# Values of one attention step and scores of the next: from one joint TensorE block to two blocks with products between

## The chip, the cores and the metric

The kernel runs on 1 core of one Trainium2 chip. The metric is device time in microseconds; before the change three timed runs took 1113.95 to 1114.95 us, median 1114.69. A core has a TensorE (PE; its weight loads are listed as PEld), a VectorE (DVE), a ScalarE (ACT), a GpSimd (POOL) and a SyncE (SP) that issues transfers. Each has its own list of instructions and works through it in order; semaphores make one wait for another.

## The reference

Three parts follow each other: an attention over chunks of 32 rows, in which each chunk sees 16 rows to its left, itself, 8 rows to its right and 8 memory rows, and two layers of products.

```python
for c in range(nc):                       # 24 chunks of 32 rows; q: (4, 8, 768, 64)
    k_ctx = k[:, :, l_start:r_end]
    v_ctx = v[:, :, l_start:r_end]
    k_full = np.concatenate([mem_k, k_ctx], axis=2)
    v_full = np.concatenate([mem_v, v_ctx], axis=2)
    scores = scale * np.matmul(q_c, k_full.transpose(0, 1, 3, 2))
    a = np.exp(scores - np.max(scores, axis=-1, keepdims=True))
    a = a / (np.sum(a, axis=-1, keepdims=True) + 1e-09)
    out[:, :, c_start:c_end] = np.matmul(a, v_full)

x = attn_out.transpose(0, 2, 1, 3).reshape(3072, 512)
h = x @ w_in                              # 512 -> 2048
x = (h * np.tanh(softplus(h))) @ w_out    # 2048 -> 512
h = x @ w2_in
return (h * sigmoid(1.702 * h)) @ w2_out
```

## The kernel before

The 3072 rows are cut into 8 blocks of 384. Attention of block j + 1 and the first product of block j are worked on at the same time. The first product is `forward`: for block j and one of 16 column tiles it multiplies in 12 matmuls of 128x384 (each operand is cut into a high and a low part, three of the four cross products are kept), L1231 in the profile. These matmuls are called products below. Behind block 7 come `across` (L1494), `first` (L1393) and `second` (L1586), which the diff doesn't touch.

For blocks 0 and 1 attention works in other functions. From block 2 on one attention step is `duo`: two pairs of heads of one block, so two steps a block and 12 in all. A step is

- scores: 48 small fp32 matmuls in tiles of 64x32 (L1059), each of which the profile shows as two matmuls and two weight loads, into the banks `s0` and `o0`;
- softmax, once for each half `hh` of the heads: a memset (L1075), a maximum (L1076) and its scaling (L1078) on DVE, six exponentials on ACT (L1083), an inverse (L802, L805) and a multiply (L1095) on DVE, three PE transposes into `s1` or `o1` (L1103), and a copy out (L1109 or L1110);
- values: 48 small fp32 matmuls in tiles of 64x64 (L1123), shown as 96, into the banks `s1` and `o1`;
- evictions: the result into the high part of the next layer's input (ACT or DVE, L1135 and L1137), and the rest into the low part (DVE, L1139).

The queries and keys of a step are turned by DVE ahead of its scores (L668, L671, L675); the loads of `v` are issued by POOL (L374) into four tiles and wait for the values that free them.

Before the change the values of a step are not an operation of their own: `duo` hands them to the next step, whose scores operation runs them first and the scores behind them, without anything between. The planner sees one operation. The first step has scores alone, the last one's values stand alone, and in between are 11 joint blocks.

The order on every engine is made by `Plan`, a list scheduler in Python: each operation has a rank (its due time, counted in products' tiles of 12 matmuls), one or two engines that can do it, and a cost in microseconds. The planner steps through a simulated time, and an engine that is free takes the ready operation with the lowest rank. The constants at the top set ranks and costs: `VAL` is the rank of values behind the step's begin, `TURN` that of the first transposes, `LATE` the distance of the second half; `COSTS` and `COSTV` are the costs of scores and values. The instructions are then written out in that order.

Of the kernel before, what the change touches and what calls it, by code (L numbers as in the profile page):

```python
# [27 lines left out]
LATE = 3  # L28
TURN = 2.7
VAL = 7.2  # L30
COSTS = 0.95
COSTV = 0.85
COSTE = 0.43


# [31 lines left out]
def fixed(t=None):  # L67

    b = Buf(None, None, None)
    b.tile = t  # L70
    return b
# [219 lines left out]
def dve(n, fast=False):  # L291
    return (155 + (0.52 if fast else 1.046) * n) / 1000


def act(n, psum=False):
    return ((172 if psum else 200) + 0.835 * n) / 1000
# [7 lines left out]
def kernel(  # L304
# [733 lines left out]
        add(r + 2.7, [("pe", 1.0 + 0.75 * (len(kept) - 1), values)], reads=reads, writes=writes)  # L1038
        evict()

    def duo(j, hp0, heads, r0, before):

        reads, writes = [x for pair in heads for x in pair], []
        cost, rank = COSTS, r0 + 0.5
        if before:
            last, rank, given, made_by, finish = before
            reads, writes, cost = reads + given, made_by, cost + COSTV
        s = [T[n].new([P, GR, 2, KEYS], F32) for n in ("s0", "o0")]

        def scores():  # L1050
            if before:
                last()
            for i, (qT, kT, _) in enumerate(heads):
                keys = kT.get().rearrange("p c d -> p (c d)")
                for c in range(NCH):
                    g, c0 = divmod(c * CHUNK, P)
                    for hh in range(2):
                        d = slice(hh * D, (hh + 1) * D)
                        nc.tensor.matmul(  # L1059
                            out=s[hh][c0:c0 + CHUNK, g, i], lhsT=qT[d, c * CHUNK:(c + 1) * CHUNK],  # L1060
                            rhs=keys[d, c * BLK:c * BLK + KEYS], start=True, stop=True, tile_position=(hh * D, c0),
                        )

        add(rank, [("pe", cost, scores)], reads=reads, writes=writes + s)
        if before:
            finish()

        vt = [values_of(j, 2 * hp0 + hh, r0) for hh in range(2)]
        left = j * TB % S == 0
        row, g, k0, n = (0, 0, 0, LEFT) if left else (P - CHUNK, GR - 1, KEYS - RIGHT, RIGHT)  # L1070

        def softmax(hh, r):
            e = T["e"].new([P, GR, 2, KEYS], F32)
            mx, sm, iv = (T[x].new([P, GR, 2], F32) for x in ("mx", "sm", "r"))
            add(r + 0.5, [("dve", 0.16, lambda: nc.vector.memset(s[hh][row:row + CHUNK, g, :, k0:k0 + n], NEG))], updates=[s[hh]])  # L1075
            add(r + 0.6, [("dve", dve(TB), lambda: nc.vector.tensor_reduce(  # L1076
                out=mx.get(), in_=s[hh].get(), axis=mybir.AxisListType.X, op=ALU.max))], reads=[s[hh]], writes=[mx])
            add(r + 0.6, [("dve", 0.16, lambda: nc.vector.tensor_scalar(  # L1078
                out=mx.get(), in0=mx.get(), scalar1=-scale, scalar2=None, op0=ALU.mult))], updates=[mx])
            done = fixed()  # L1080

            def power(g, i):
                nc.scalar.activation(  # L1083
                    out=e[:, g, i], in_=s[hh][:, g, i], func=AF.Exp, scale=scale,
                    bias=mx[:, g, i:i + 1], accum_out=sm[:, g, i:i + 1],
                )

            for g_ in range(GR):
                for i in range(2):
                    add(  # L1090
                        r + 1, [("act", COSTE, lambda g=g_, i=i: power(g, i))],
                        reads=[s[hh], mx], writes=[done, sm, e], table="exp",
                    )
            inverses(r, sm, iv)
            add(r + 1.4, [("dve", dve(TB), lambda: nc.vector.tensor_tensor(  # L1095
                out=e.get(), in0=e.get(), in1=iv.get().unsqueeze(3).to_broadcast([P, GR, 2, KEYS]), op=ALU.mult,
            ))], reads=[iv, done], updates=[e])
            t = T[("s1", "o1")[hh]].new([P, TB], F32)
            aT = T["aT"].new([P, TB], F32)

            def turn():
                for g in range(GR):
                    nc.tensor.transpose(  # L1103
                        t[:, g * P:(g + 1) * P], e[:, g].rearrange("p i k -> p (i k)"), ident.get()
                    )

            add(r + TURN, [("pe", 0.43, turn)], reads=[e, ident], writes=[t])
            add(r + TURN + 0.2, [
                ("act", act(TB, True), lambda: nc.scalar.activation(out=aT.get(), in_=t.get(), func=AF.Copy)),  # L1109
                ("dve", dve(TB), lambda: nc.vector.tensor_copy(out=aT.get(), in_=t.get())),  # L1110
            ], reads=[t], writes=[aT])
            return aT

        aT = [softmax(hh, r0 + LATE * hh) for hh in range(2)]
        o = [T[n].new([P, TB], F32) for n in ("s1", "o1")]

        def values():
            for c in range(NCH):
                cs = slice(c * CHUNK, (c + 1) * CHUNK)
                for hh in range(2):  # L1120
                    for i in range(2):
                        d = slice(i * D, (i + 1) * D)
                        nc.tensor.matmul(  # L1123
                            out=o[i][hh * D:(hh + 1) * D, cs], lhsT=vt[hh][d, c], rhs=aT[hh][d, cs],
                            start=True, stop=True, tile_position=(i * D, hh * D),
                        )

        def evict():
            if j not in x0:
                x0[j] = Inputs("xh", j), Inputs("xl", j)  # L1130
            xh, xl = x0[j]
            for i in range(2):
                hp, part = hp0 + i, fixed()
                add(r0 + VAL + 0.2, [
                    ("act", act(TB, True), lambda hp=hp, i=i: nc.scalar.activation(  # L1135
                        out=xh.at(hp), in_=o[i].get(), func=AF.Copy)),
                    ("dve", dve(TB), lambda hp=hp, i=i: nc.vector.tensor_copy(out=xh.at(hp), in_=o[i].get())),  # L1137
                ], reads=[o[i]], writes=[xh.buf(hp), part])
                add(r0 + VAL + 0.4, [("dve", dve(TB), lambda hp=hp, i=i: nc.vector.tensor_tensor(  # L1139
                    out=xl.at(hp), in0=o[i].get(), in1=xh.at(hp), op=ALU.subtract))],  # L1140
                    reads=[o[i], part], writes=[xl.buf(hp)])

        reads = [*vt, *aT]
        if (j, hp0) != (NB - 1, H // 2 - 2):
            return values, r0 + VAL, reads, o, evict
        add(r0 + VAL, [("pe", COSTV + 0.1, values)], reads=reads, writes=o)
        evict()

    def quads():

        last, todo, before = None, [], None
        for j in range(NB):
            if j == EARLY:
                more = [T[x].new([P, 2 * DM], F32) for x in ("wo15", "wo11", "wo12", "wo13", "wo14")]
# [15 lines left out]
            for n in range(NQ):  # L1170
                rank = base + 2 * n
                if j == 0:
                    gp, hp = divmod(n, H // 2)
                    if hp == 0:
                        st = rows_of_heads(j, gp, rank)
                    heads, vals = turned(j, hp, gp, st, rank), st[2]
                else:
                    hp, gp = divmod(n, GB // 2)
                    if gp == 0:
                        if j >= EARLY:  # L1180
                            todo.append(pair_of_heads(j, hp, rank - 4 * (hp % 2)))
                            if hp % 2:
                                before = duo(j, hp - 1, todo, rank - 4, before)
                                todo = []
                            yield
                            continue
                        if hp == 0:
                            st = [rows_of_heads(j, i, rank) for i in range(GB // 2)]
                        pair = [turned(j, hp, i, st[i], rank) for i in range(GB // 2)]
                        names = (("s0", "s1"), ("o0", "o1"))[hp % 2]  # L1190
                        s = oct_scores([pair], rank, [names])[0]
                        both = [T[x].new([GQ, GB, 2], F32) for x in ("sm", "r")]
                        es = [quad(j, hp, i, pair[i], rank + STAGGER * i, s, both) for i in range(GB // 2)]
                        inverses(rank + STAGGER, *both)
                        for _, scaled in es:
                            scaled()
                        oct_out(j, rank, [x[2] for x in st], [(hp, names, [e for e, _ in es], 0)])
                    yield
                    continue
# [536 lines left out]
```

## Time and profile before

| | |
|---|---|
| median of three timed runs | 1114.69 us |
| profiled execution, its own time | 1113.29 us |
| its span (first to last instruction) | 1111.5 us |
| PE busy | 1079.9 us (97%) |
| DVE busy | 796.3 us (72%) |
| ACT busy | 552.4 us (50%) |
| mean granted clock of PE | 0.994 of full speed |

A stretch of the views is given in microseconds from the first instruction. In rows of busy time by stretch the columns are the stretch, its length, the busy time and the count of instructions of PE, PEld, DVE, ACT and POOL, the granted clock of PE as a share of full speed, the share of the DMA engines' time, and GB/s. In rows in order of time they are the start, the length, the engine, the line and operation, the tiles written and read. In the chain of waits a row is a piece of the chain that ended last, and "issue" is time in which the engine waited for nothing that the profile shows. A row of waits names the engine and line that waited, what it waited for, the total, the number of times and the longest.

### The profile page before, as it was taken

The numbers are of one execution on the slowest core, as the hardware profiler recorded it, in microseconds if no ns is written. First come the engines' busy times: TensorE is split into PE (matmuls) and PEld (weight loads), VectorE is DVE, ScalarE is ACT, GpSimd is POOL, SyncE is SP. The second block draws the span as 40 slices with busy tenths as digits, with TensorE's granted clock in tenths as the row PEclk, the third lists the DMA queues.
The fourth block names the chain that finished last, engine by engine and source line by source line (L and its number), as shares of the span: only waits on it lengthen the run. The fifth ranks groups of instructions, "written<-read, shape, count | busy, mean of one in ns | idle before, by whom it ended". The sixth has DMA issues, their size and how long they took to land.

```text
span 1111.5 us, 24805 instructions
## 1 busy us (share of the span) xinstructions
PE 1079.9 (97%) x9642; PEld 1045.3 (94%) x9642; DVE 796.3 (72%) x1457; ACT 552.4 (50%) x1247; POOL 98.4 (9%) x167
## 2 busy tenths in 40 slices
PE   7899899999999999999999999999999999999998
PEld 6568898998999999999999999999999999999998
DVE  5995654746545698898879865667556787877875
ACT  5874444444454464655555556555565533333332
POOL 2006443235300000000000000000000000000000
PEclk9999999999999999999999999999999999999999
DMA  9988998789876764754642777868678636445361
GB/s 178 274 233 211 250 224 232 202 226 243 239 246 233 249 190 159 252 162 136 220 146 83 223 244 239 289 219 285 212 251 253 182 101 171 115 125 151 104 162 48
DMA packets 278732, 221.28 MB, mean 199 GB/s; under 512 B 113552, under 2 KB 253867, under 8 KB 278615
## 3 DMA queue, kind: packets, MB, share of 16 engines
q1 hardware_dynamic: 272055, 209.46, 64.2%
q0 software_dynamic: 6560, 10.24, 3.7%
q8 instruction: 76, 1.25, 0.5%
q14 instruction: 41, 0.34, 0.1%
HBM read 138.33 MB, written 81.26 MB: 198 GB/s over the span
## 4 chain that ended last, share of the span: by engine, by line
PE 85%; DMA 5%; DVE 5%; issue 2%; SPq 2%; ACT 1%; DVEq 0%; ACTq 0%
PE o L1231 13%; PE h L1231 12%; PE o L1586 9%; PE o L1494 8%; PE h L1393 8%; PE o L1393 6%; PE h L1586 6%; PE s L1494 6%; PE s L1586 5%; PE h L1494 5%; PE s L1393 3%; DMA st<-wd 2%; SPq L374 2%; PE s L1123 1%; PE s L1059 1%
## 5 line engine op out<-in xcount | busy, mean ns | idle before, releaser
L1231 PE MATMUL o<-xh,wi 128*128 128x384 f32 x320 | 85.0, 347 | 0.0
L1231 PE MATMUL h<-xh,wi 128*128 128x384 f32 x320 | 82.4, 338 | 0.0
L1231 PEld LDWEIGHTS o<-xh,wi 128*128 128x128 f32 x320 | 58.1, 192 | 0.7 <-issue 0.3
L1231 PEld LDWEIGHTS h<-xh,wi 128*128 128x128 f32 x320 | 57.7, 188 | 0.6 <-ACT z L1363 0.2
L1231 PE MATMUL o<-xl,wi 128*128 128x384 f32 x160 | 54.5, 341 | 0.0
L1231 PE MATMUL h<-xl,wi 128*128 128x384 f32 x160 | 53.7, 336 | 0.0
L1363 ACT ACTIVATE e<-h 128x384 f32<-128x384 f32 (+2 forms) x47 | 22.4, 476 | 46.8 <-PE h L1586 28.8
L1586 PE MATMUL o<-wo,xh 128*128 128x256 f32 x232 | 43.7, 282 | 0.0
L1576 DVE TENSOR_TENSOR xl<-vt,xh 128x1024 fp32r<-128x1024 f32 x24 | 29.4, 1223 | 19.6 <-ACT xh L1573 17.5
L1576 DVE TENSOR_TENSOR xl<-wi,xh 128x1024 fp32r<-128x1024 f32 x32 | 38.8, 1223 | 5.8 <-ACT xh L1573 5.0
L1494 PE MATMUL o<-xh,wo 128*128 128x256 f32 x224 | 40.5, 282 | 0.0
L1231 PE MATMUL o<-wo,wi 128*128 128x384 f32 x192 | 38.7, 351 | 0.0
L374 POOL DMA_DIRECT2D vt<-in_v_dram x50 | 32.4, 652 | 64.5 <-PE o L1123 33.0
L1573 ACT ACTIVATE xh<-wi 128x1024 fp32r<-128x1024 f32 x25 | 26.4, 1057 | 22.8 <-DMA wi<-gd 12.5
L374 POOL DMA_DIRECT2D wo<-in_v_dram x50 | 32.0, 644 | 65.1 <-PE o L1123 64.4
L1477 DVE TENSOR_TENSOR xl<-z,xh 128x1024 fp32r<-128x1024 f32 x24 | 29.3, 1223 | 9.5 <-ACT xh L1473 8.9
L1586 PEld LDWEIGHTS o<-wo,xh 128*128 128x128 f32 x232 | 36.0, 190 | 0.0
L1231 PE MATMUL h<-wo,wi 128*128 128x384 f32 x192 | 35.1, 337 | 0.0
L1231 PEld LDWEIGHTS o<-wo,wi 128*128 128x128 f32 x192 | 34.6, 196 | 0.4
L1494 PEld LDWEIGHTS o<-xh,wo 128*128 128x128 f32 x224 | 34.6, 190 | 0.0
L1363 ACT ACTIVATE ev<-o 128x384 f32<-128x384 f32 (+2 forms) x32 | 15.1, 471 | 39.1 <-PE o L1586 17.2
L1231 PEld LDWEIGHTS h<-wo,wi 128*128 128x128 f32 x192 | 33.7, 189 | 0.0
(462 smaller groups left out, 3502.2 us busy)
## 6 DMA issues: line engine op xcount, KB each, us to landing
st<-in_moe_w_out_dram SPq DMA_DIRECT2D x32, 512.0 KB
st<-wd SPq DMA_DIRECT2D x29, 512.0 KB
z<-g1d SPq DMA_DIRECT2D x24, 512.0 KB
vt<-gd SPq DMA_DIRECT2D x24, 512.0 KB
wi<-gd SPq DMA_DIRECT2D x24, 512.0 KB
g1d<-gl SPq DMA_DIRECT2D x46, 192.0 KB
g1d<-z SPq DMA_DIRECT2D x45, 192.0 KB
wi<-in_moe_w_in_dram SPq DMA_DIRECT2D x16, 512.0 KB
```

What stands on the lines that cost most here:

```text
L374: queue.dma_start(out=o, in_=i)
L1059: nc.tensor.matmul(out=s[hh][c0:c0 + CHUNK, g, i], lhsT=qT[d, c * CHUNK:(c + 1) * CHUNK], rhs=keys[d, c * BLK:c * BLK + KEYS], start=True, ...
L1123: nc.tensor.matmul(out=o[i][hh * D:(hh + 1) * D, cs], lhsT=vt[hh][d, c], rhs=aT[hh][d, cs], start=True, stop=True, tile_position=(i * D, h ...
L1231: nc.tensor.matmul(out=h.get(), lhsT=a[:, c], rhs=b.at(kk), start=(n == 0), stop=(n == KD * len(prods) - 1))
L1363: ("act", act(n, True), lambda: nc.scalar.activation(out=dst(), in_=bank.get(), func=AF.Copy)),
L1393: nc.tensor.matmul(out=bank.get(), lhsT=a, rhs=b, start=(fresh and m == 0), stop=(m == 3 * K2 - 1), skip_group_check=not fresh,)
L1477: add(rank + 0.05, [("dve", dve(n2), lambda gh=gh, gl=gl, src=src: nc.vector.tensor_tensor(out=flat(gl), in0=flat(src), in1=flat(gh), op=A ...
L1494: nc.tensor.matmul(out=bank[:, d, :], lhsT=a, rhs=b[:, p, :], start=(fresh and h == d == p == m == 0), stop=(h == 1 and p == HP - 1 and m ...
L1573: ("act", act(NP * P), lambda: nc.scalar.activation(out=flat(gh), in_=flat(src), func=AF.Copy)),
L1576: add(rank + 0.05, [("dve", dve(NP * P), lambda: nc.vector.tensor_tensor(out=flat(gl), in0=flat(src), in1=flat(gh), op=ALU.subtract))], re ...
L1586: nc.tensor.matmul(out=bank.get(), lhsT=a[:, p], rhs=b, start=(fresh and p == 0 and m == 0), stop=(p == NP - 1 and m == 2), skip_group_che ...
```

## The change

`duo` gets the values and their evictions as operations of its own, at rank `VAL` behind the step's begin, and its scores at rank `SCORE` = 1.5 behind it instead of 0.5 or, joined with the values before them, at those values' rank. The costs are 1.05 for scores and 1.75 for values, instead of 0.95 and 0.85, 1.80 for a joint block. Nothing is computed otherwise.

```diff
-COSTS = 0.95
-COSTV = 0.85
+SCORE = 1.5
+COSTS = 1.05
+COSTV = 1.75
...
-    def duo(j, hp0, heads, r0, before):
-
-        reads, writes = [x for pair in heads for x in pair], []
-        cost, rank = COSTS, r0 + 0.5
-        if before:
-            last, rank, given, made_by, finish = before
-            reads, writes, cost = reads + given, made_by, cost + COSTV
+    def duo(j, hp0, heads, r0):
+
+        reads = [x for pair in heads for x in pair]
         s = [T[n].new([P, GR, 2, KEYS], F32) for n in ("s0", "o0")]
 
         def scores():
-            if before:
-                last()
             for i, (qT, kT, _) in enumerate(heads):
...
-        add(rank, [("pe", cost, scores)], reads=reads, writes=writes + s)
-        if before:
-            finish()
+        add(r0 + SCORE, [("pe", COSTS, scores)], reads=reads, writes=s)
...
-        reads = [*vt, *aT]
-        if (j, hp0) != (NB - 1, H // 2 - 2):
-            return values, r0 + VAL, reads, o, evict
-        add(r0 + VAL, [("pe", COSTV + 0.1, values)], reads=reads, writes=o)
-        evict()
+        add(r0 + VAL, [("pe", COSTV, values)], reads=[*vt, *aT], writes=o)
+        if j not in x0:
+            x0[j] = Inputs("xh", j), Inputs("xl", j)
...
-                                before = duo(j, hp - 1, todo, rank - 4, before)
+                                duo(j, hp - 1, todo, rank - 4)
```

Through ranks and costs the planner's order changes on all engines between the first scores and the first rows of `across`. In the new kernel scores are L1054, transposes L1096, values L1116 and products L1218.

PE before, in the middle of the joint block of the fifth and sixth step (at 178 to 184 us in the trace): the last values of one step (L1123) and the first scores of the next (L1059).

```order
L1123 MATMUL s_2534<-z_267,vt 64x32
L1123 MATMUL o_2536<-z_267,vt 64x32
L1059 MATMUL s_2584<-wo_945 32x64
L1059 MATMUL o_2586<-wo_945 32x64
L1059 MATMUL s_2584<-wo_945 32x64
```

PE now, at the same two blocks: the last values, the products (L1218) of two column tiles, the first scores.

```order
L1116 MATMUL o_2491<-z_267,vt 64x32
L1218 MATMUL h<-wo_1504,wi_942 128x384 x2
L1218 MATMUL h<-wo_1510,wi_942 128x384
...
L1218 MATMUL h<-wo_1753,wi_984 128x384 x2
L1218 MATMUL h<-wo_1760,wi_984 128x384
L1054 MATMUL s_2593<-wo_945 32x64
L1054 MATMUL o_2595<-wo_945 32x64
```

24 products stand between the two now; so it is in eight places.

PE now, between the first values (L1116) and the third scores (L1054).

```order
L1116 MATMUL o_1440<-z_267,vt 64x32
L1218 MATMUL h<-xh,wi_697 128x384 x2
L1218 MATMUL h<-xl,wi_697 128x384
L1218 MATMUL h<-xh,wi_697 128x384 x2
L1218 MATMUL h<-xl,wi_697 128x384
L1054 MATMUL s_1513<-wo_945 32x64
```

Only 6 products stand here. The second scores moved to between the first step's two groups of transposes.

PE now, between the third values and the fourth scores.

```order
L1116 MATMUL s_1865<-z_267,vt 64x32
L1116 MATMUL o_1867<-z_267,vt 64x32
L1054 MATMUL s_1922<-z_152 32x64
L1054 MATMUL o_1924<-z_152 32x64
L1054 MATMUL s_1922<-z_152 32x64
```

At this place the planner still puts the scores right behind the values.

DVE before, behind the scores of that sixth step: the memsets (L1075), the low parts of the values before (L1139), the two maxima (L1076).

```order
L1137 CAST xh<-s_2534 128x384
L1075 MEMSET s_2584 32x2x16
L1075 MEMSET o_2586 32x2x16
L1139 TENSOR_TENSOR xl<-s_2534,xh 128x384
L1139 TENSOR_TENSOR xl<-o_2536,xh 128x384
L1076 TENSOR_REDUCE mx<-s_2584 128x6
L1076 TENSOR_REDUCE mx<-o_2586 128x6
```

DVE now, at the same place (L1130 and L1132 are the evictions, L1068 the memsets, L669 and L672 transposes of later queries and keys, L1069 the maxima).

```order
L1130 CAST xh<-o_2491 128x384
L1132 TENSOR_TENSOR xl<-s_2489,xh 128x384
L1132 TENSOR_TENSOR xl<-o_2491,xh 128x384
L669 STREAM_TRANSPOSE z_152<-z_136 128x384
L1068 MEMSET s_2593 32x2x16
L1068 MEMSET o_2595 32x2x16
L672 STREAM_TRANSPOSE wo_945<-wo_383 128x13x32
L1069 TENSOR_REDUCE mx<-s_2593 128x6
L1069 TENSOR_REDUCE mx<-o_2595 128x6
```

The evictions moved from between memset and maximum to ahead of the memsets.

## Rows read from the trace of the kernel before

**Rows 1.** The page: busy times; the instruction queue's packets, MB, share
```profile
PE 1079.9 (97%) x9642; PEld 1045.3 (94%) x9642; DVE 796.3 (72%) x1457; ACT 552.4 (50%) x1247; POOL 98.4 (9%) x167
...
q8 instruction: 76, 1.25, 0.5%
```

**Rows 2.** Busy by stage: stretch, length, PE, PEld, DVE, ACT, POOL, clock, DMA share
```profile
88.00:330.00 242.00, 231.09 (x3433) 223.06 (x3432) 138.61 (x377) 110.99 (x424) 91.34 (x150) 0.98 0.89 232
...
520.00:1111.50 591.50, 584.51 (x4266) 581.97 (x4265) 432.00 (x609) 279.55 (x480) 0.00 (x0) 1.00 0.59 181
```

**Rows 3.** What PE waited for, 88 to 332 us: total, times, longest
```profile
PE s L1059 <- issue: 7.4, 4, 2.5
PE o L1059 <- issue: 3.5, 3, 1.5
```

**Rows 4.** Chain of waits, two joint blocks: start us, us, what
```profile
119.47 0.17 PE s L1123
121.37 2.17 issue
...
124.44 3.32 PE o L1231 x18
...
158.02 0.17 PE s L1123
...
160.66 2.28 PE o L1231 x12
```

**Rows 5.** Busy time and instruction counts between stalls, columns as in rows 2
```profile
108.33:119.30 10.97, 10.97 (x127) 10.68 (x126) 8.46 (x26) 5.59 (x29) 7.07 (x13) 1.00 1.07 242
119.30:123.54 4.24, 2.07 (x126) 1.78 (x126) 0.56 (x1) 0.49 (x1) 1.51 (x3) 1.00 0.96 245
178.80:183.15 4.35, 1.81 (x138) 1.62 (x130) 0.56 (x1) 0.87 (x2) 3.17 (x6) 1.00 0.96 241
247.63:250.24 2.61, 1.95 (x141) 1.76 (x133) 0.56 (x1) 0.87 (x2) 1.06 (x2) 1.00 0.40 89
183.15:250.24 67.09, 66.43 (x886) 64.91 (x885) 40.73 (x105) 31.89 (x117) 20.58 (x35) 0.97 0.81 209
```

**Rows 6.** Chain of waits: products behind three stalls, behind values alone, later
```profile
140.44 2.22 PE o L1231 x6
...
183.57 3.84 PE o L1231 x12
...
269.58 3.58 PE o L1231 x12
...
330.12 4.36 PE o L1231 x24
334.48 4.16 PE h L1231 x24
```

**Rows 7.** Busy time and granted clock behind the stall that ended at 139.15
```profile
140.44:142.66 2.22, 2.22 (x7) 2.22 (x8) 2.16 (x8) 0.00 (x0) 2.06 (x4) 0.50 1.29 182
```

**Rows 8.** Chain of waits: first products behind three steps' scores
```profile
109.21 4.38 PE o L1231 x24
...
205.41 2.30 PE o L1231 x12
...
313.88 1.25 PE o L1231 x6
```

**Rows 9.** Order of time on DVE, five places: start us, us, instruction
```profile
93.66 0.20 DVE L675 COPY wo<-z 128x96 f32<-128x96 f32 x1
...
114.11 0.20 DVE L675 COPY z<-z 128x96 f32<-128x96 f32 x1
...
205.41 0.55 DVE L1139 TENSOR_TENSOR xl<-o,xh 128x384 fp32r<-128x384 f32 x1
...
210.56 0.56 DVE L1095 TENSOR_TENSOR e<-e,r 128x384 f32<-128x384 f32 x1
...
325.52 0.56 DVE L1095 TENSOR_TENSOR e<-e,r 128x384 f32<-128x384 f32 x1
```

More of the change, by code (lines that the diff above doesn't have):

```diff
@@ L1126, in values @@
                         )
[L1128 to L1141, printed above, removed]
-        reads = [*vt, *aT]
-        if (j, hp0) != (NB - 1, H // 2 - 2):
-            return values, r0 + VAL, reads, o, evict
-        add(r0 + VAL, [("pe", COSTV + 0.1, values)], reads=reads, writes=o)
-        evict()
+        add(r0 + VAL, [("pe", COSTV, values)], reads=[*vt, *aT], writes=o)
+        if j not in x0:
+            x0[j] = Inputs("xh", j), Inputs("xl", j)
+        xh, xl = x0[j]
+        for i in range(2):
+            hp, part = hp0 + i, fixed()
+            add(r0 + VAL + 0.2, [
+                ("act", act(TB, True), lambda hp=hp, i=i: nc.scalar.activation(
+                    out=xh.at(hp), in_=o[i].get(), func=AF.Copy)),
+                ("dve", dve(TB), lambda hp=hp, i=i: nc.vector.tensor_copy(out=xh.at(hp), in_=o[i].get())),
+            ], reads=[o[i]], writes=[xh.buf(hp), part])
+            add(r0 + VAL + 0.4, [("dve", dve(TB), lambda hp=hp, i=i: nc.vector.tensor_tensor(
+                out=xl.at(hp), in0=o[i].get(), in1=xh.at(hp), op=ALU.subtract))],
+                reads=[o[i], part], writes=[xl.buf(hp)])
     def quads():
-        last, todo, before = None, [], None
+        last, todo = None, []
         for j in range(NB):
```

## The prediction

> **What bounds the kernel now.** I read the page's busy line, then the busy time by stage, then what TensorE (PE) waits for in the stage that changes, then the chain of waits through that stage, and last the instruction counts between its stalls.
>
> PE is busy 97% of the span [rows 1]. By stage it is busy 231.1 of 242.0 us between 88 and 330 us, where the changed blocks run, and 584.5 of 591.5 us from 520 us to the end [rows 2]. So microseconds that PE loses or gains between 88 and 330 us go to the end nearly one for one, unless something else becomes late. What PE waits for in that stage is one thing: 10.9 us (7.4 + 3.5) in seven pieces, all at the scores' matmuls of L1059 and all called "issue" [rows 3]. No piece is a wait for data.
>
> The chain shows where such a piece lies. One joint block begins with values at 119.47, goes over to scores, and in the middle of the scores PE stands for 2.17 us; products go on at 124.44. The undisturbed block goes from 158.02 to 160.66, 2.64 us, against 4.97 here [rows 4]. There are 11 joint blocks; 7 have such a stall and 4 do not, as the seven pieces say.
>
> The stalls have a period. Between the stall that ends at 108.33 and the one that ends at 123.54, PE ran 127 + 126 and 126 + 126 matmuls and weight loads, and between those that end at 183.15 and 250.24 there are 886 + 885 [rows 5]: 253, 252 and 7 x 253. The page's instruction queue moved 76 packets and 1.25 MB, and PE alone has 2 x 9642 such instructions [rows 1], which is 254 a packet. So I take it that PE stands because the next packet of its own instructions has not come: a stall sits at a packet's boundary. Counted on in this way along PE's list, eight of the 11 joint blocks meet two boundaries, one just ahead of the block or in its values and one in its scores; seven of these eight stall, and the three blocks with one boundary don't. How long a packet takes after the boundary before it: 252 instructions took 4.24 us with the stall, in other blocks 4.35 and 2.61 us [rows 5]. A joint block is 384 matmuls and weight loads in 2.64 us, so a whole packet is used up there in under 2 us; products (24 in 4.16 us [rows 6]) use one up in 22 us.
>
> The Trainium skill, "Runtime: NRT & Kernel Launch", section on instruction fetch mechanics, names blocks of 16 KiB (256 instructions), which fits the count, and calls the cost of crossing one "mostly hidden". By that sentence the stalls would not be fetches, the change would win nothing and the time would be that of the first rival below; the trace disagrees with it here, with 10.9 us in seven pieces.
>
> **What the change removes.** Values and scores become two blocks. In PE's new list 24 products stand between them in eight of the eleven places, 6 in one and none in one; the second values stand alone among products. The price of the stalls, all of it:
> - standing: 10.9 us [rows 3].
> - restart: the block above is 2.33 us longer than the undisturbed one, of which 2.17 is standing; 0.16 x 7 = 1.1 us.
> - clock: behind three stalls the granted clock is down, in the one shown 0.50, the 1.2 GHz level [rows 7]. Twelve products take 3.84 and 3.58 us and six take 2.22, against 2.28 for twelve behind the undisturbed block [rows 4, 6] (six: 2.28 less six at 4.16/24, 1.24). Lost: 1.56 + 1.30 + 0.98 = 3.8 us.
>
> Sum 15.8 us. Which of it stays follows from where the boundaries fall in the new list, counted on in packets from the first scores, up to which PE's list is unchanged. With 24 products between, the shortest way from one boundary to the next holds 4.16 us of products and about 1.3 us of small matmuls, 5.5 us, over the longest packet time seen (4.35). Two places are shorter. With 6 products between (first values, third scores) a packet holds some 124 instructions of values, 6 products and 119 of scores, about 2.9 us: a wait of 0 to 1.5 us, I take 0.7. Where values and scores still touch (third values, fourth scores) it holds 174 and 82, about 1.85 us: a wait of 0 to 2.5 us, I take 1.4, the mean of the eight old blocks with two boundaries (10.9 / 8), and add 0.16 for the restart and 0.55 for the clock (three of seven stalls lost 1.3 each). Stays: 2.8 us.
>
> **What it adds.** A seam each time PE goes from small tiles back to products: behind values that stand alone 24 products take 4.36 us instead of 4.16 [rows 6], 0.2 us; going in shows no extra piece in the chain. Ten new seams, 2.0 us.
>
> **What it moves.** PE's work is otherwise the same, and so are the instructions of VectorE (DVE) and ScalarE. Two moves matter.
>
> First, the softmax has less time. Until now 42 to 54 products stood between the scores and their first transpose; now 36 in four steps (6.2 us, with the seam 6.4) and 42 to 54 in the next five, with 12 or 6 more before the second transpose (8.9 us behind the scores in the four steps, 9.9 to 11.0 in the five). The DVE multiply that the first transpose needs ended 5.7 us behind the scores in an undisturbed step (205.41 to 210.56 + 0.56), and the slowest second one 12.2 us behind (313.88 to 325.52 + 0.56) [rows 8, 9]. So the bounds are no wait at all and, if every second multiply were as slow as that one, 3.3 x 4 + 2.3 + 2.2 + 1.2 x 3 = 21.3 us. But in the old list the evictions of the joint block's values stood ahead of the reduce on DVE; in the new one they come 24 products earlier, which takes two subtractions of 0.55 us out of the softmax's way [rows 9]. The undisturbed row is the nearer one, and its slack is 0.7 us: I take 1.0 us for all nine steps.
>
> Second, early scores move forward. The second scores stand right behind the first step's first transposes now, and behind the first values the third scores come after 6 products (1.0 us) instead of after the second scores, 54 products, transposes and the second values (1.1 + 9.4 + 0.6 + 1.5 us): 11 to 12 us sooner each. Their DVE copies ended at 93.86 and 114.31 in the old run [rows 9]. The third's overwrite tiles that the second scores read until 109.21 [rows 8], so it was PE that dated them; now those tiles are free that much sooner. Cost 0, at most about 5 us (114.31 against the 109 at which the third scores now come due) if the loads are the true date, and no gain is in it, since PE has products to do meanwhile.
>
> DMA must bring the same bytes in a stage 10 us shorter: 0.89 of 242 us [rows 2] becomes 0.93. No PE wait there is for a load, so I cost it at nothing; if the cover is gone the stage can give back no more than it won.
>
> **Sum.** 15.8 - 2.8 - 2.0 - 1.0 = 10.0 us faster. The profiled execution took 1113.29 us, its span 1111.5; the difference of 1.8 lies around it. It stands 1.4 us below the median of the three timed runs, 1114.69. 1113.29 - 10.0 = 1103.3 for such a run, 1104.7 for the median. This leaves PE's waits behind the stage as they are.
>
> **Rivals.**
> - The stalls are not PE's instructions, or PE's queue delivers them as late in any order (the change doesn't do what it says). For it: four joint blocks run without one. Against it: the period of 253, and that the blocks without a second boundary never stall. Then nothing goes, seams and waits are added: 1114.7 + 2.0 + 1.0 = 1117.7. Chance 0.05. The skill's "mostly hidden" would come out here too.
> - Fetches get slower, or more boundaries fall badly than I count, and half of the stalls stay: 1114.7 - 7.9 + 3.0 = 1109.8. Chance 0.08.
> - Loads date the third and fourth scores: up to 5 us come back, 1110. For it: DMA is at 0.89 of the stage and the scores are pulled forward by 12 us. Against it: no PE or DVE wait for a load there. Chance 0.12.
> - Slower: PE waits for the softmax. Place: the second transpose of the nine steps from the fourth scores on; price, if each second multiply ends as late as the slowest shown, the 21.3 us above in place of my 1.0: 1114.7 - 11.0 + 21.3 = 1125. It decides from 1.2 us a step (11.0 / 9). For it: 0.7 us of slack is little, and DVE takes other work between the softmax's instructions. Against it: the evictions leave the way, the slowest row is that of one step only, the last, and PE has no such wait now [rows 3]. Chance 0.05.
>
> **How the numbers follow.** The forecast has 0.70; its own range is 1100 (no stall stays and no wait is added: 1114.7 - 15.8 + 2.0 = 1100.9) to 1109. The two rivals at 1110 hold 0.20 more, and with them the range is 1100 to 1112. A change under 0.2% (2.2 us) can't be told from none by a measurement of this kernel. Faster: 0.70 + 0.08 + 0.12, less 0.05 for both of these together, which would eat the gain: 0.85. Same: those 0.05. Slower: the first rival and the last, 0.10.
>
> **What would show it.** Right: PE's "issue" waits between 88 and 330 us fall from 10.9 to 1 to 4 us, and the rest sits where 6 products or none separate the blocks; the granted clock in the stage rises from 0.98 to 0.99 or more; 24 products more stand behind the last values now, so these end about 14 us earlier, near 316 us; products behind a block alone take 0.2 us more. Wrong: "issue" pieces with 24 products around them; PE waiting at L1096 (the new transposes) for DVE, or at L1054 for DVE's copies; or the last values early and the end not, which would put the loss into the waits behind 330 us.

## The result, and the profile after

The changed kernel takes 1103.5 us (median of six runs, 1101.3 to 1105.1), the kernel before 1114.8 beside it (1113.3 to 1117.6). The ratio is 0.990, 95% interval 0.988 to 0.991: faster by 11.3 us; a second measurement (experiment 7) has 0.993, 7.3 us. Predicted were 1104.7 us and a range of 1100 to 1112. The profiled execution of after took 1105.1 us, the longest of the six, its span 1103.3.

The page of after, its busy line and its instruction queue; they answer [rows 1].

```profile
PE 1079.3 (98%) x9642; PEld 1041.1 (94%) x9642; DVE 800.3 (73%) x1456; ACT 555.8 (50%) x1246; POOL 98.6 (9%) x169
...
q8 instruction: 76, 1.25, 0.5%
```

PE has the same instructions and the same busy time to 0.6 us, in a span 8.2 us shorter. Busy time by stretch in after, columns as in [rows 2]. The first row is the stage, from the first scores to the end of the products before the last values; the three others answer to [rows 5] and run from one packet boundary to the next, with 277, 277 and 282 matmuls and weight loads begun or running in them (254 to 256 begin there, the others were still running).

```profile
89.91:318.98 229.07, 223.67 (x3313) 212.62 (x3312) 141.49 (x376) 113.47 (x423) 91.38 (x152) 1.00 0.92 246
108.52:112.27 3.75, 3.09 (x142) 2.65 (x135) 3.72 (x10) 1.37 (x3) 2.37 (x4) 1.00 0.87 170
133.26:136.37 3.11, 2.06 (x139) 1.88 (x138) 1.59 (x3) 1.34 (x3) 1.36 (x3) 1.00 0.63 208
299.20:305.27 6.07, 5.83 (x145) 5.37 (x137) 3.56 (x7) 2.59 (x5) 0.00 (x0) 1.00 1.08 380
```

The granted clock of the stage is 1.00 now, against 0.98, and DMA is at 0.92 against 0.89 [rows 2]. What PE waited for between 84 and 332 us in after; it answers [rows 3]: line, releaser, total, times, longest.

```profile
PE s L1096 <- DVE e L1088: 1.5, 1, 1.5
PE s L1054 <- issue: 1.3, 2, 1.0
PE o L1096 <- ACT z L1350: 1.0, 1, 1.0
PE o L1096 <- DVE e L1088: 0.8, 2, 0.5
PE o L1054 <- issue: 0.7, 1, 0.7
```

The unexplained "issue" falls from 10.9 us in seven pieces to 2.0 in three. In its place PE waits 3.3 us at the transposes (1.5 + 1.0 + 0.8), where it did not wait before. The chain of waits of after shows the three pieces and, at its end, the products behind the last values; it answers [rows 4, 6].

```profile
109.63 1.25 PE h L1218 x6
...
111.61 0.66 issue
...
133.20 0.17 PE s L1116
...
134.73 0.17 PE s L1054
...
135.32 1.05 issue
...
305.03 0.24 issue
...
320.58 4.36 PE h L1218 x24
324.95 4.16 PE o L1218 x24
```

The piece of 0.66 us stands in the scores behind the place with 6 products, that of 1.05 where values (133.20) run into scores (134.73) without a product, and that of 0.24 at a place with 24 products.

What such a piece waits for can also be read directly, since the trace lists the transfers of the instruction queue: 76 packets of 16 KB in a run. The rows show that queue from 121.00 to 122.10 us in before, ahead of the stall that ends at 123.54, and from 302.80 to 303.90 us in after, ahead of the piece that ends at 305.27 (packets, MB, share of the DMA engines' time).

```profile
q8 instruction: 1, 0.02, 5.8%
```

```profile
q8 instruction: 1, 0.02, 5.6%
```

No other packet of the queue begins between the packet boundary ahead of the stall and the stall's end. The first packet takes 1.02 us and ends at 122.05, the second takes 0.98 us and ends at 303.85; PE goes on 1.49 and 1.41 us later. The same holds for all 32 pieces of "issue" in the stage in the twelve profiles of this case: PE goes on 1.2 to 1.6 us after the end of such a packet, though packets come only every 9 us or so there. So PE stands for its own instructions, and not only the period says so.

Last, PE's waits from 332 us on: the five rows of before, then the three of after.

```profile
PE s L1586 <- DVE xl L1576: 1.6, 1, 1.6
PE s L1494 <- DVE xl L1477: 1.5, 1, 1.5
PE s L1494 <- DVE wi L1477: 0.8, 1, 0.8
PE h L1393 <- DVE v L1406: 0.7, 2, 0.4
PE h L1393 <- ACT h L1363: 0.2, 1, 0.2
```

```profile
PE s L1573 <- DVE xl L1563: 2.0, 1, 2.0
PE o L1481 <- DVE xl L1464: 0.2, 1, 0.2
PE o L1573 <- DVE xl L1563: 0.2, 1, 0.2
```

They fall from 4.8 to 2.4 us; the prediction had left them as they were.

### The profile page after: what moved, and what is told of

It reads as the page before. It is cut to its first block, busy times and chain, and to the rows that moved or that the text cites. A ratio compares the mean times of both kernels' runs of the same rounds, so it can differ in the third digit from the quotient of the medians.

```text
span 1103.3 us, 24808 instructions
## 1 busy us (share of the span) xinstructions
PE 1079.3 (98%) x9642; PEld 1041.1 (94%) x9642; DVE 800.3 (73%) x1456; ACT 555.8 (50%) x1246; POOL 98.6 (9%) x169
## 4 chain that ended last, share of the span: by engine, by line
PE 78%; DMA 10%; DVE 5%; SPq 4%; issue 1%; ACT 1%; DVEq 0%; ACTq 0%
PE o L1481 9%; PE o L1573 9%; PE h L1218 9%; PE o L1218 8%; PE h L1380 7%; PE o L1380 6%; PE s L1481 6%; PE h L1573 6%; PE h L1481 6%; PE s L1573 5%; SPq L375 4%; PE s L1380 3%; DMA st<-wd 3%; DMA st<-in_moe_w_out_dram 2%; DMA g1d<-ev 1%
## 5 line engine op out<-in xcount | busy, mean ns | idle before, releaser
L1218 PE MATMUL h<-xh,wi 128*128 128x384 f32 x320 | 82.9, 340 | 0.0
L1218 PE MATMUL o<-xh,wi 128*128 128x384 f32 x320 | 82.7, 339 | 0.0
L1218 PEld LDWEIGHTS h<-xh,wi 128*128 128x128 f32 x320 | 57.2, 188 | 0.6
L1218 PEld LDWEIGHTS o<-xh,wi 128*128 128x128 f32 x320 | 57.0, 188 | 0.5
L1218 PE MATMUL h<-xl,wi 128*128 128x384 f32 x160 | 53.7, 336 | 0.0
L1218 PE MATMUL o<-xl,wi 128*128 128x384 f32 x160 | 53.7, 336 | 0.0
L1218 PE MATMUL o<-wo,wi 128*128 128x384 f32 x192 | 36.2, 340 | 0.0
L1218 PE MATMUL h<-wo,wi 128*128 128x384 f32 x192 | 35.7, 339 | 0.0
L1218 PEld LDWEIGHTS h<-wo,wi 128*128 128x128 f32 x192 | 33.2, 188 | 0.2
L1218 PEld LDWEIGHTS o<-wo,wi 128*128 128x128 f32 x192 | 33.0, 188 | 0.4
```

What stands on the lines that cost most here:

```text
L1218: nc.tensor.matmul(out=h.get(), lhsT=a[:, c], rhs=b.at(kk), start=(n == 0), stop=(n == KD * len(prods) - 1))
```

## The experiments

Two theories stood against each other at first. The prediction's: PE stands for the next packet of its own instructions where a packet is used up faster than the next one comes, and products between the small blocks give the time. The rival: the stalls are of another kind, and the new costs and order do the rest.

**1. The new costs, the joint block kept** (kernel before).

```diff
-COSTS = 0.95
-COSTV = 0.85
+COSTS = 1.05
+COSTV = 1.75
```

> The kernel before with one thing of the change: the new costs (1.05 and 1.75, so 2.80 for a joint block) and so another order of the planner; values and scores stay one joint block. Theory (PE stands for the next packet of its instructions when two boundaries fall into one joint block): counted on along the new list, eight of the eleven joint blocks again have two boundaries less than 4.2 us of work apart, together 14.1 us short of 4.2 us where the kernel before has 18.0; so about 14.1/18.0 of its 15.8 us stay, PE's issue waits at the scores come to 7 to 10 us, and the time is 1109 to 1114 us. Rival (the gain came from the planner's other order and costs, not from splitting): 1102 to 1105 us and issue waits under 3 us.

Measured: 1110.7 us (before 1114.0 in these rounds), ratio 0.9985, interval 0.9966 to 1.0003. PE's waits between 84 and 332 us:

```profile
PE s L1103 <- DVE e L1095: 3.9, 1, 3.9
PE o L1059 <- issue: 3.5, 2, 2.0
PE s L1103 <- ACT gl L1363: 1.9, 1, 1.9
PE s L1059 <- issue: 1.6, 1, 1.6
PE h L1231 <- issue: 1.1, 1, 1.1
```

Costs and order alone do not make the gain. They do two other things: 5.8 us of waits at the transposes appear (the first and the third row) with the blocks still joint, and `across` no longer waits behind the stage (only 2.8 us are left there, all in `first` and `second`). Issue is 6.2 us, a little under what was expected.

**2. The kernel before, its list shifted by 32 instructions** through eight more matmuls at the start.

```diff
-WARM = 16
+WARM = 24
```

> The kernel before with 24 instead of 16 warm-up matmuls at its start: everything in PE's list stands 32 matmuls and weight loads later, and nothing else is changed. Theory: the packet boundaries fall elsewhere in the joint blocks. By the count two boundaries are now 1.8 to 2.1 us apart in the 4th, 5th, 8th and 11th joint block, which stall by 1.5 to 2.5 us each, and 3.5 to 4.7 us apart in the 1st, 2nd, 3rd, 6th, 7th, 9th and 10th, which stall by under 1 us or not at all (before: 1st, 2nd, 3rd, 5th, 8th, 9th and 11th stalled, the 4th did not). The work that is short of 4.2 us is 11.1 us instead of 18.0, so 6 us of the 15.8 go, less up to 3 us if the longer warm-up delays the first stage: 1108 to 1112 us. Rival (the scores' small matmuls stand for a reason of their own, in these blocks): the same blocks stall, 1114 to 1118 us.

Measured: 1109.3 us, ratio 0.9967 (0.9951 to 0.9984). Nothing in the stage is changed, and yet some of the stalls move to other blocks. PE's waits in the stage:

```profile
PE s L1059 <- issue: 5.0, 2, 3.4
PE o L1059 <- issue: 2.0, 2, 1.4
PE o L1231 <- issue: 0.9, 1, 0.9
```

The first three joint blocks, which stalled before, run through now, and the products behind the fourth, which did not, stand (0.9 us). The fifth, eighth, ninth and eleventh stall in both, and the ninth stands 3.4 us, more than any before, where under 1 us was expected; products run at half clock behind it. Its packet began 5.1 us behind the boundary ahead of it. Counted from the start of PE's list, the four stalls common to both profiles stand behind the same number of recorded matmuls and weight loads (3959, 5727, 6231 and 7495), although the work there moved by 32. So a stall belongs to a place in PE's list and not to the work that stands there.

**3. and 10. More distance: scores ranked later** (kernel after; twice, in different rounds).

```diff
-SCORE = 1.5
+SCORE = 2.0
```

> The changed kernel with the scores' rank at 2.0 instead of 1.5 behind the step's begin. By the list 36 products now stand between values and scores in most steps, at least 18 in all, and no two boundaries are less than 4.7 us of work apart. Theory: PE's issue waits at scores and values fall from 2.0 us to under 0.5, which gives 1.5 to 2.5 us: 1101 to 1102 us, if PE's waits for the softmax at the transposes stay at about 3.3 us. Rival (what is left in the changed kernel is the softmax's distance, and fewer products between its transposes and the values cost more): waits at the transposes grow to 5 us or more, 1104 to 1107 us.

> The changed kernel with SCORE 2.0 a second time, beside the two others on the same chip: issue under 0.5 us, waits at the transposes 3 to 5 us, VectorE's waits for transfers in the stage 12 to 20 us; time 1101.5 to 1104.5.

Measured: 1103.0 us, ratio 0.9908 (0.9886 to 0.9930), and 1103.7 us, ratio 0.9907 (0.9879 to 0.9935). With 36 products between values and scores behind the fourth scores, and 18 at each of the two short places of after, no issue wait is left in the stage, in either profile. PE's waits there in the first of the two are the whole of this:

```profile
PE s L1096 <- DVE wo L1132: 1.6, 1, 1.6
PE s L1096 <- ACT ev L1350: 1.2, 1, 1.2
PE o L1096 <- DVE e L1088: 0.5, 1, 0.5
```

The last 2.0 us of issue are gone as expected, but the medians do not show it; from the first scores to the end it is 1012.0 and 1012.2 us, against 1013.4 in after. The waits at the transposes stay, 3.3 and 4.6 us.

**4. and 6. Less distance** (kernel after; the second for a profile, since the first profile stood 6 us below its median).

```diff
-SCORE = 1.5
+SCORE = 0.5
```

> The changed kernel with the scores' rank at 0.5, its rank before the change. By the list 12 products stand between values and scores in most steps, in the other order too (scores, 12 products, values), and none at one place; two boundaries are 1.8, 2.6 and 3.5 to 4.7 us of work apart in nine places. Theory: the distance decides, so there are pieces of issue at most of these nine places, the two short ones 1.5 to 2.5 us, the others 0 to 1 us, together 3 to 7 us, and the time is 1104 to 1108 us. Rival (any products between are enough): issue waits as in the changed kernel, 2 us, 1103 to 1104 us.

> The changed kernel with SCORE 0.5 a second time, for its profile: its median of 1111.9 stood 6 us above its profiled execution. Theory (the same short distances between packet boundaries, 12 or no products, are met with fetch times that differ from execution to execution): where this execution takes 1109 to 1114, the issue waits between the first scores and the last values are 8 to 12 us instead of 5.0, at five to nine places whose distance between boundaries is under 5 us. Rival (the loss lies elsewhere): issue waits stay near 5 us and the rest shows behind 330 us or before the first scores.

Measured: 1111.9 us, ratio 0.9985 (0.9964 to 1.0006), single runs from 1103 to 1117; the second profile 1112.1. PE's waits in the stage, of the second profile:

```profile
PE s L1096 <- DVE r L803: 4.3, 1, 4.3
PE s L1116 <- issue: 2.6, 1, 2.6
PE h L1218 <- issue: 2.3, 1, 2.3
PE o L1116 <- issue: 1.2, 1, 1.2
```

With two blocks as in after, but 12 products or none between them in most steps, the gain is gone. Issue was 5.0 us in the first profile, as expected, and 6.1 in the second, where 8 to 12 were expected: longer waits for packets explain 1.1 of the 6.4 us between the two. The larger piece is one wait at a transpose, 4.3 us, which the first profile does not have: neither what I took for the cause of the spread nor, in the main, a loss behind the stage (0.6 us more there). At its end the granted clock falls to 0.50 for 3.4 us, one such stretch more than in the first profile.

**5. Second transposes later** (kernel after).

```diff
-TURN = 2.7
-VAL = 7.2
-SCORE = 1.5
+TURN = 4.0
+VAL = 8.2
+SCORE = 2.5
```

> The changed kernel with SCORE 2.5, VAL 8.2, TURN 4.0 instead of 1.5, 7.2, 2.7: nothing computed otherwise. 24 products stand between values and the next scores (12 and 18 at the first two places), none touch, and the second transposes stand 48 to 60 products behind the scores instead of 48 to 54 mostly. Theory (packets need distance, softmax needs time): PE's issue waits in the stage at most 0.7 us, waits at the transposes fall from 3.3 to about 1.5 us, mostly at the first transposes, which stay 36 to 42 products behind the scores; time 1100 to 1102.5. Rival (the waits at the transposes come from DVE's order and not from the distance): transposes still wait 3 us or more, time 1102 to 1104.

Measured: 1106.9 us, ratio 0.9943 (0.9923 to 0.9963): slower than expected by either. No issue is left in the stage, and the transposes wait 6.1 us, one of them 4.5. More distance did not help; the rival named VectorE's order, and the chain of waits showed a load behind it: the load lands at 229.47, VectorE stands for it and works through the pieces next in its list, and the multiply for the transposes begins only at 232.84. That became the second question.

**7. The changed kernel again, beside 5 and 6.**

> The changed kernel itself, on the same chip as the others: 1102.5 to 1104.5, issue waits in the stage 1 to 3 us at the two places without 24 products between, waits at the transposes 2.5 to 4 us, a third small stall with 24 products only in some executions (0 to 0.6 us).

Measured: 1105.6 us, ratio 0.9934 (0.9911 to 0.9957), 1 us above the range expected (before takes 1112.9 here); its interval touches that of the first measurement (0.988 to 0.991). Issue is 1.6 us in two pieces, at the places with 6 products and none; the third is not there. Again one transpose waits long, 3.5 us. The chain of waits leads from it back to a load:

```profile
219.41 10.47 DMA st<-in_moe_w_in_dram
...
229.91 0.66 ACT u L416
...
230.59 0.04 DVE u L425
...
230.94 0.56 DVE e L1088
...
231.63 0.82 PE s L1096 x3
```

The load of a weight tile lands at 229.88 (219.41 + 10.47). ScalarE, which has that tile's conversion (L416) in its list between the exponentials, stands for it; VectorE has its next piece (L425) ahead of the softmax's multiply (L1088) and stands for ScalarE; PE's transposes stand for the multiply. The softmax itself had all it needed. Behind this wait TensorE's granted clock is 0.50, the 1.2 GHz level, for 3.4 us (columns as in [rows 2]); the first profile of after, whose longest wait is 1.5 us, has no such stretch in the stage.

```profile
231.70:235.10 3.40, 3.40 (x12) 3.40 (x13) 2.86 (x7) 1.77 (x6) 0.00 (x0) 0.50 0.68 143
```

Counted over 88 to 330 us, VectorE waits for transfers 20.5 us in after and ScalarE 17.2 (16.8 and 23.1 in this second profile), against 0 and 1.6 in the kernel before, and 23.3 and 34.3 in experiment 1. The two longest rows of VectorE's in after:

```profile
DVE z L632 <- DMA z<-in_mem_k_dram: 4.0, 1, 4.0
DVE v L478 <- DMA wd<-v: 2.7, 2, 1.4
```

Theory from here on: the new costs make a step longer in the planner's time (2.80 us for scores and values instead of 1.80), while its loads take what they took; so it puts the users of loads among earlier products than the chip has loaded for.

**8. Loads planned to land later** (kernel after, also SCORE 2.0).

```diff
-LANDING = 3.5
-SCORE = 1.5
+LANDING = 5.0
+SCORE = 2.0
```

> The changed kernel with SCORE 2.0 and with the planner's lag for a load at 5.0 us instead of 3.5 (LANDING): loads' users are placed later in the order of every engine; 30 to 36 products between values and next scores, 12 at one place. Theory (what is left of waits at the transposes comes from VectorE and ScalarE standing in their lists for loads that a faster TensorE now overtakes): VectorE's waits for transfers between 88 and 330 us fall from 14 to 20 us to under 10, ScalarE's from 9 to 23 to under 10, TensorE's waits at the transposes to under 2 us, issue under 1 us; time 1100 to 1102.5. Rival (the transfers themselves are the limit of the stage, so a later place of their users only moves the wait): the waits for transfers stay, or TensorE waits at scores or products; time 1103 to 1106.

Measured: 1103.3 us, ratio 0.9912 (0.9888 to 0.9936). Half a miss: VectorE's waits for transfers fall to 7.5 us, but ScalarE's stay, 24.8 us, 13.4 of them at L416, and the transposes wait 5.4 us. My reading, not tested further: a lag of 1.5 us more does not undo a step that is 1 us too long eleven times over.

**9. Two blocks with the old costs** (kernel after).

```diff
-SCORE = 1.5
-COSTS = 1.05
-COSTV = 1.75
+SCORE = 3.0
+COSTS = 0.95
+COSTV = 0.85
```

> The changed kernel with the old costs (COSTS 0.95, COSTV 0.85) and SCORE 3.0: values and scores are two blocks with products between at every place but one (none there), in an order that differs on all engines. Theory (the new costs stretch the planner's stage by about 11 us against the loads, so that VectorE and ScalarE meet their loads too early): their waits for transfers between 88 and 330 us fall to under 8 us each, TensorE's waits at transposes to under 2 us, issue 0 to 2 us; time 1100 to 1103. Rival (a faster stage waits for its loads in any order): waits for transfers stay at 14 us or more on VectorE; time 1103 to 1106.

Measured: 1101.9 us, ratio 0.9891 (0.9864 to 0.9919), the lowest median of all, but not distinguishable from after's 0.990, and with an interval that touches after's second one. PE's waits in the stage, all of them:

```profile
PE o L1116 <- issue: 1.3, 1, 1.3
PE o L1054 <- issue: 0.6, 2, 0.4
PE o L1218 <- DVE ev L1351: 0.5, 1, 0.5
```

VectorE's waits for transfers in this kernel, also all of them:

```profile
DVE v L425 <- DMA g1d<-z: 2.1, 1, 2.1
DVE z L672 <- DMA z<-in_k_dram: 1.1, 1, 1.1
DVE z L669 <- DMA z<-in_k_dram: 1.0, 1, 1.0
```

No transpose waits. Transfers are waited for 4.2 us on VectorE and 2.9 on ScalarE, at a DMA share of 0.93, above after's; so the transfers are not the limit of a stage this fast, their users stood too early in the lists. The rival of 8 and 9 falls. With experiment 1 (joint blocks, new costs, many such waits) the costs are the likely cause from both sides, and the split is not needed for these waits. One thing is left open: SCORE differs too. 3, 5 and 10 change SCORE under the new costs and keep the waits, but the first profile of experiment 4 (SCORE 0.5, new costs) waits for transfers only 4.3 us on VectorE and 8.1 on ScalarE, its second 13.8 and 18.1; experiment 9 has one profile.

The wins are partly handed back: 4.0 us of waits behind the stage (`across` again among them) and 1.9 us of issue. The longest of those pieces stands behind 24 products, at a place that the prediction would have called safe:

```profile
115.51 4.38 PE h L1218 x24
...
120.58 1.30 issue
```

From the boundary ahead of it (114.55) to the end of the piece it is 7.3 us; the packet began only at 119.38.

## Why the prediction was right

The forecast was 10.0 us; the medians give 11.3 us, and 7.3 us in experiment 7. From the first scores (88.04 before, 89.91 after) to the end of the span the profiles differ by 10.1 (1023.5 and 1013.4). Its terms beside what the two profiles show:

| term | predicted | measured |
|---|---|---|
| standing removed | 10.9 - 2.1 = 8.8 | 10.9 - 2.0 = 8.9 |
| restarts removed | 0.9 | 0.6 (four stalls fewer, at the predicted 0.16) |
| half clock removed | 3.8 - 0.55 = 3.3 | 3.8 (the price of before; none left in the stage) |
| ten seams | -2.0 | -2.0 (0.20 at the last values) |
| waits at the transposes | -1.0 | -3.3 |
| waits behind the stage | 0 | +2.4 |
| sum | 10.0 | 10.4 |

- **That the stalls are PE's own instructions, and that distance removes them**, held. The stalls keep their place in the list when the work is shifted (experiment 2), are gone in four profiles with at least 12 products at every place, mostly 24 to 36 (3, 5, 8, 10), and come back in the split kernel when the distance is taken away (4, 6). In all profiles they stand at the same place, to within six, of a period of 252 to 253 recorded matmuls and weight loads, and end 1.2 to 1.6 us after a packet of PE's instructions has come in. Distance does not remove all of them: experiment 9 has 1.3 us behind 24 products.
- **What stays** was placed right: 0.66 us at the 6 products (I took 0.7) and 1.05 where the blocks touch (I took 1.4). The third piece, 0.24 us, has 24 products before it, which the prediction named as a sign against it. The step that failed: "the longest packet time seen (4.35)" was taken as the longest there is. That packet of after lasted 6.07 us with 0.46 between the starts of two of its matmuls, so it took longer than I allowed; in the second profile of the same kernel the same place took 5.58 us and nothing stood. There is no fixed time from boundary to boundary. In experiment 9 intervals of 5.92, 6.36 and 7.33 us held pieces of 0.4, 0.2 and 1.3 us; on the other side 1.76 us ran through in before (202.72 to 204.47), 2.08 to 2.68 in experiment 1 and 3.86 in experiment 8 (boundaries counted on along the recorded list). The packets ahead of the 32 pieces took only 0.9 to 1.7 us each; what varied is when they began, from 0.5 us ahead of the boundary before to 5.1 us behind it. Why some begin late no run shows. In these runs more distance made stalls rarer, and 24 products did not exclude one.
- **The seam** is the 4.36 against 4.16 us of the last values' products in after, and the "x24" rows at 299 and 305 us read alike (4.36 and 4.39); this price was right.
- **The softmax waits are the mis-sized term**: 3.3 us for 1.0 (4.5 in the second profile). The bounds of 0 to 21.3 us held it, but for another reason than I weighed. I weighed the distance between scores and transposes, where the slack was 0.7 us. What ended late was mostly the multiply, and behind it stood a load (experiment 7; in after the longest wait leads back to a load that landed at 226.40, with pieces of VectorE's list between the two). The prediction had this in two halves that it kept apart: the rival "loads date the third and fourth scores", which did not happen (no wait at L1054 for a copy), and "no PE or DVE wait for a load there", which was true of before only. In a stage 10 us shorter that runs from lists planned with longer steps, the loads were met at other places: by VectorE and ScalarE, inside the softmax. Where such a wait is long, it costs clock as well, which no term had.
- **The waits behind the stage** were left as they were and fell by 2.4 us. Experiment 1 shows the waits of `across` gone with the costs alone, and with the old costs in experiment 9 one of them is back. So the costs, which I priced at nothing, took 2 to 3 us at the transposes and gave about as much back behind the stage; that the sum fits so closely is partly luck.
- **The last values** were expected to end near 316 us; the products behind them begin at 320.58. Of the 4.6 us, 1.9 is that the first scores themselves began later in this execution, and 2.3 that the transposes waited more.

By the Trainium skill, "Runtime: NRT & Kernel Launch", section on instruction fetch mechanics, the cost of a boundary is "mostly hidden". The runs agree at most boundaries. They disagree at 32 places in twelve profiles, most of them where small matmuls use a packet up quickly: up to 2.5 us of standing in the kernel before [rows 3] and 3.4 us in experiment 2.

## What to carry to other kernels

Many tiny matmuls in a row can run out of instructions: if an engine near 100% shows "issue" waits in the middle of such a run, count the instructions between the waits and see when the instruction queue's packets came in, and if the count is regular, spread the small ones among large ones rather than look for a missing operand. When a planner's cost is changed to move one engine's work, look at every engine's waits afterwards: its costs are also the clock by which users of loads are placed, and a cost that is too long puts them ahead of their loads. And when a stage gets shorter, ask of each load what it is late for now, not only whether it was late before.

## What had not been expected of the hardware

- Eight matmuls more at the start made the whole kernel before 0.3% faster (experiment 2, 1109.3 us), and from the first scores on its list differs only in where packets end. Differences of this size between two versions can be such a shift.
- The packets of PE's instructions ahead of the 32 pieces took 0.9 to 1.7 us to come, and PE went on 1.2 to 1.6 us after their end; but they began up to 5.1 us after the boundary ahead, so 24 products (4.2 us) between small blocks hid the wait in most places and not in all.
- Single runs scatter by several us, with stalls or without: the kernel before went from 1108.3 to 1118.1 us in one set of 29 and experiment 4 across 14 us in 12; experiment 5, whose profile has no issue wait, across 10 us in 12, and experiments 3 and 10, one kernel, across 3 and 7 us in six each.
- The same wait has another length in the next execution: the longest wait at the transposes was 1.5 us in one profile of after and 3.5 in the other, at the same step.
